# The causal mask of a row-maximum pass, added on TensorE with 64-column identities and 16-bit constants

## The chip, the cores and the metric

The kernel runs on one core of one Trainium2 chip. The metric is the device time of one execution in microseconds (us). Before the change it is 672.27 us, the median of three runs (671.01 to 672.72).

## The reference, cut to what matters

The layer mixes two branches by a per-token gate. Branch A is attention over 2048 tokens in four segments of 512, with 32 heads of 20 channels; within a segment it is causal softmax attention, and across segments a memory of keys and values is read. Branch B sends one token through a feed-forward network. What the change touches is the causal logits:

```python
mask = (ar[:, None] < ar[None, :]).astype(x.dtype) * (-1e9)
logits = jnp.einsum("bhqd,bhkd->bhqk", qs, ks) * scale + mask
p = _softmax(logits, axis=-1)
a_dot = jnp.einsum("bhqk,bhkd->bhqd", p, vs)
```

Softmax needs the maximum of each row of the masked logits. Key j is hidden from query i when i < j.

## The kernel before, in words

Work is cut into 8 units (two halves of the heads, `NU`, times four segments) and each unit into four groups of four heads, so 32 groups n. Per unit, `projections` makes the keys, queries and values by products of split operands (a high and a low part in float32r, a 32-bit type that TensorE reads with fewer bits), at line 371 in `pair_up`: two products at a time, one in rows 0 to 63 of the array, one in rows 64 to 127. They go through DRAM (`place`, `place_low`, `bring_back`) into stacked tiles `qs` and `ks`, where two heads lie in each half of the partitions.

For each group there are two passes over the logits, in five steps k = 0 to 4 each (`LOGITS` lists which blocks of 128 queries and how many keys a step has).

- The first pass, `a_step` (line 645), finds the row maxima. TensorE writes the logits of a step, queries on the partitions, into the one PSUM tile `a` (line 653). Then the mask is added for the last 128 keys of each block of queries, where the diagonal lies (lines 656 to 663). VectorE (DVE) reduces `a` to maxima (lines 666 and 670), which frees `a` for the next step. After k = 4, `m_split` and `m_rows` (line 697) turn the negated maxima into two rows that are put beside the queries.
- The second pass, `b_step` (line 710), makes the transposed logits less the maxima (line 717); ScalarE (ACT) takes the exponential (line 721), GpSimd (POOL) clears what lies above the diagonal (line 727), and `pv_step` multiplies by the values (line 742). `norm` (line 769) divides and stores. `memory_read` (line 503), `memory_write` (line 527) and `keys` (line 492) serve the memory.

The mask of a block is a product of two constants. `pick[r, h]` and `tri[r, h]` lie in the partitions of row half r (64 partitions). With q for a query's and t for a key's place in the block, the rows of h stand for queries 64h to 64h + 63: `pick` as weights has a 1 where a row stands for query q, and `tri`, streamed, holds -1e30 where t is beyond the row's query. The two rounds h = 0 and 1 add up to the mask over all 128 queries, and b = 0, 1 are the two halves of the partitions, each with its own PSUM bank. For k = 0, 1 one block is masked (128 columns streamed, line 660), for k = 2, 3, 4 two blocks in one product (256 columns, line 662). So each step has four mask products, with four loads of weights.

The order of the work is made by a planner while the program is written out: it keeps an estimate of each engine's clock (`now`) and chooses the next piece for TensorE from what should be ready (`a_step`, `b_step`, a piece of projection, `pv_step`, chores). Its costs are constants, such as the step of the maxima:

```python
end = pe((0.41, 0.41, 0.49, 0.49, 0.46)[k], free["a"], stack(n))
```

The change leaves these constants as they are. Each engine then runs its instructions in that order.

`constants` (line 103) fills the constant tiles once, near the start, behind the first splits of weights: an iota on POOL gives `jp` (column less partition), and DVE makes `identf` (line 108), `pick` (line 118) and `tri` (line 119) from it. Behind these, in DVE's order, stand the first copy of a projection out of PSUM (line 428) and more splits (line 175).

Of the kernel before, what the change touches and what calls it, by code (L numbers as in the profile page):

```python
# [8 lines left out]
F32R = mybir.dt.float32r  # L9
BF16 = mybir.dt.bfloat16  # L10
I32 = mybir.dt.int32
AF = mybir.ActivationFunctionType
OP = mybir.AluOpType
# [21 lines left out]
NEG = -1e30  # L35
# [17 lines left out]
def sub(ap, off, dims):  # L53
    return bass.AP(tensor=ap.tensor, offset=ap.offset + off, ap=[list(ap.ap[0])] + dims)
# [3 lines left out]
def tile_infini_mod(  # L58
# [12 lines left out]
    nc = tc.nc  # L71
    one = ctx.enter_context(tc.tile_pool(name="one", bufs=1))
# [10 lines left out]
    def f32(t):  # L83
        return t.bitcast(F32)
# [2 lines left out]


    identf = one.tile([128, 128], F32, name="identf")
    pick = one.tile([128, 2, 128], F32R, name="pick")  # L90
    tri = one.tile([128, 2, 128], F32R, name="tri")
    gate = one.tile([128, H], F32, name="gate")
    ogate = one.tile([128, H], F32, name="ogate")
    mask4 = one.tile([GC, 4], F32, name="mask4")
# [8 lines left out]
    def constants():  # L103
        for t in mneg:
            nc.gpsimd.memset(f32(t), 0.0)
        jp = pool.tile([128, 4 * GW], I32, tag="num", bufs=6, name="jp")[:, :128]
        nc.gpsimd.iota(jp, pattern=[[1, 128]], base=0, channel_multiplier=-1)
        nc.vector.tensor_scalar(identf, jp, 0.0, None, op0=OP.is_equal)
        for i, t in enumerate(ks):
            (nc.gpsimd if i % 2 else nc.vector).memset(f32(t), 1.0)  # L110
        for t in va:
            nc.gpsimd.memset(t, 1.0)

        for h in range(2):
            for r in range(2):
                p = slice(64 * r, 64 * r + 64)
                off = 64.0 * (h - r)
                nc.vector.tensor_scalar(pick[p, h], jp[p], off, None, op0=OP.is_equal)
                nc.vector.tensor_scalar(tri[p, h], jp[p], off, NEG, op0=OP.is_gt, op1=OP.mult)
        nc.sync.dma_start(gate, bass.AP(tensor=beta.tensor, offset=beta.offset, ap=[[0, 128], [1, H]]))  # L120
        nc.scalar.activation(gate, gate, AF.Exp, scale=-1.0)
        nc.vector.tensor_scalar(gate, gate, 1.0, None, op0=OP.add)
        nc.vector.reciprocal(gate, gate)
        nc.vector.tensor_scalar(ogate, gate, -1.0, 1.0, op0=OP.mult, op1=OP.add)

        jd = pool.tile([128, 4 * GW], I32, tag="num", bufs=6, name="jd")[:GC, :GC].rearrange("p (a b) -> p a b", a=4)
        nc.gpsimd.iota(jd, pattern=[[1, 4], [4, DH]], base=0, channel_multiplier=-1)
        ed = pool.tile([128, 4 * GW], F32, tag="num", bufs=6, name="ed")[:GC, :GC].rearrange("p (a b) -> p a b", a=4)
        nc.vector.tensor_scalar(ed, jd, 0.0, None, op0=OP.is_equal)
        nc.vector.tensor_reduce(out=mask4, in_=ed, axis=AX.X, op=OP.max)  # L130
        run("POOL", 4.5)
        run("DVE", 5.5)
# [4 lines left out]
    def run(engine, us, *ready):  # L137
        now[engine] = max([now[engine], *(r + 0.12 for r in ready)]) + us
        return now[engine]

    def pe(us, *ready):
        now["PE"] = max([now["PE"], *ready]) + us
        return now["PE"] + 0.22
# [196 lines left out]
    def use(m):  # L340
        if mode[0] != m:
            mode[0] = m
            pe(0.22)
# [301 lines left out]
    def a_step(n, k):  # L645
        use((64, 128))
        if n not in mx:
            mx[n] = pool.tile([128, 2, 2, 4], F32, tag="mx", bufs=3, name="mx")
        a = psum.tile([128, 2, 512], F32, tag="a", bufs=1, name="a")
        for i, p, at, w in LOGITS[k]:  # L650
            for b in range(2):
                q_ = qs[n % NS][64 * b:64 * b + ST, p, 128 * i:128 * i + 128]
                nc.tensor.matmul(a[:, b, at:at + w], q_, ks[n % NS][64 * b:64 * b + ST, p, :w],  # L653
                                 start=(i, p) == LOGITS[k][0][:2], stop=False)
        ends = [at + w - 128 for i, p, at, w in LOGITS[k]]
        for h in range(2):
            for b in range(2):
                r = slice(64 * b, 64 * b + 64)
                if k < 2:
                    nc.tensor.matmul(a[:, b, ends[0]:], pick[r, h], tri[r, h], start=False, stop=h == 1)  # L660
                else:
                    nc.tensor.matmul(sub(a[:, b], min(ends), [[max(ends) - min(ends), 2], [1, 128]]), pick[r, h],  # L662
                                     sub(tri[r, h], 0, [[0, 2], [1, 128]]), start=False, stop=h == 1)
        end = pe((0.41, 0.41, 0.49, 0.49, 0.46)[k], free["a"], stack(n))
        if k == 4:
            nc.vector.tensor_reduce(out=mx[n][:, :, :, 1], in_=a.rearrange("p b (c t) -> p b c t", c=2), axis=AX.X, op=OP.max)  # L666
            end = run("DVE", 0.16 + 2 / 0.96 * 0.512, end)
        else:
            for i, p, at, w in LOGITS[k]:
                nc.vector.tensor_reduce(out=mx[n][:, :, p, i:i + 1], in_=a[:, :, at:at + w], axis=AX.X, op=OP.max)  # L670
                end = run("DVE", 0.16 + w / 480, end)
        free["a"] = end + 0.1
        done_a[0] += 1
        if k == 4:
            m_split(n)

    def stack(n):
        return max(landed.get(("q", n), 1e9), landed.get(("k", n), 1e9))

    def m_split(n):  # L680
        m = mx.pop(n).rearrange("p b c i -> p b (c i)")
        t = mneg[n % 2]
        hi, lo = sub(t, 0, [[16, 2], [1, 8]]), sub(t, 8, [[16, 2], [1, 8]])
        nc.vector.tensor_scalar(hi, m, -1.0, None, op0=OP.mult)
        nc.vector.scalar_tensor_tensor(out=lo, in0=m, scalar=-1.0, in1=f32(hi), op0=OP.mult, op1=OP.subtract)  # L685
        rows.append((run("DVE", 0.5), n))
# [418 lines left out]
    def logits(ahead, t):  # L1105

        best = None
        for fn, e in ((a_step, next_a()), (b_step, next_b())):
            if e and e[1] <= t and e[0] + LEAD <= chunks[0] + ahead and (best is None or e[0] < best[1][0]):
                best = fn, e  # L1110
        if best is None:
            return False
        fn, e = best
        if fn is b_step:
            b_no[0] += 1
        fn(e[2], e[3])
        return True
# [21 lines left out]
    for _ in range(9):  # L1139
        split_next()  # L1140
    constants()
    now["PE"] = at["T", 0, 0]
    last_side = [0.0]
# [94 lines left out]
```

## Time and profile before

| What | Value |
|---|---|
| median of three runs | 672.27 us |
| profiled execution | 670.66 us |
| its span, first to last instruction | 668.3 us |
| granted TensorE clock | 0.984 |
| TensorE matmuls busy | 618.0 us |
| TensorE weight loads busy | 497.9 us |
| VectorE, ScalarE, GpSimd busy | 401.5, 366.6, 278.3 us |

How to read it: PE is TensorE's matmuls, PEld its weight loads, which overlap them; DVE, ACT, POOL and SP are VectorE, ScalarE, GpSimd and SyncE. A row of groups gives the line, the engine, the operation, the tiles written and read, the shape, the count, then the busy time in us and the mean duration of one in ns, then the idle time of the engine before them and what ended it. A shape such as 64*128 64x256 is 64 rows of the array by 128 columns of weights, with 64 partitions by 256 elements streamed or written. A row of the timeline gives the start and the duration in us, and merges like instructions that follow each other (x4). Matmuls overlap, so that a duration is a latency; what a product costs is read from the distance between starts.

### The profile page before, as it was taken

To read this page: it belongs to the slowest core of one execution; us is meant where nothing else is said; L and a number is where in the kernel's file an instruction comes from. 1 tells how busy PE (TensorE), PEld (TensorE's weight loads), DVE (VectorE), ACT (ScalarE), POOL (GpSimd) and SP (SyncE) were. 2 spreads that over 40 slices of the span, in tenths; PEclk is the share of its full clock that TensorE was granted. 3 is DMA by queue.
4 is the path that set the end of the run, shared out by engine and by line. 5 is a ranking of instruction groups with operands and counts; after the bars stand their busy time and mean duration, and the time that the engine had idled before them with its cause. 6 is when DMAs were issued, how large, how long until landed. Compare 5 with 4: busy or idle time off the path is not lost.

```text
span 668.3 us, 17482 instructions
## 1 busy us (share of the span) xinstructions
PE 618.0 (92%) x6996; PEld 497.9 (75%) x6996; DVE 401.5 (60%) x675; ACT 366.6 (55%) x638; POOL 278.3 (42%) x350
## 2 busy tenths in 40 slices
PE   4589899999999889899999999999999999999996
PEld 3478777788887676776777787777777788787785
DVE  6635665656765747665647684766667676663332
ACT  6452575556756665576346744656465555555331
POOL 5443332633454645554423436343457433232211
PEclk9799989999999979899999999999999999999999
DMA  6598557345642677488847884578625793344451
GB/s 178 163 268 232 162 137 221 101 121 162 168 107 73 196 213 186 135 264 260 258 140 228 260 217 130 144 230 246 192 59 160 222 277 94 116 140 135 140 182 60
DMA packets 81319, 116.55 MB, mean 174 GB/s; under 512 B 36112, under 2 KB 41752, under 8 KB 81240
## 3 DMA queue, kind: packets, MB, share of 16 engines
q1 hardware_dynamic: 81240, 115.46, 59.5%
q8 instruction: 55, 0.90, 0.6%
q14 instruction: 24, 0.20, 0.1%
HBM read 72.94 MB, written 41.96 MB: 172 GB/s over the span
## 4 chain that ended last, share of the span: by engine, by line
PE 73%; DVE 10%; DMA 6%; issue 4%; SPq 2%; ACT 2%; POOL 2%; POOLq 0%; ACTq 0%; DVEq 0%
PE sums L371 23%; PE sumt L371 14%; PE pv L742 10%; PE a L653 5%; PE bt L717 5%; PE a L662 4%; PE nm L503 3%; SPq L147 2%; PE otp L769 2%; DVE mx L666 2%; DMA stkk<-lo 2%; PE mp L527 2%; DMA stkk<-hi 2%; PE a L660 1%; DVE mneg L685 1%
## 5 line engine op out<-in xcount | busy, mean ns | idle before, releaser
L721 ACT ACTIVATE p<-bt 128x1024 f32<-128x1024 f32 x160 | 164.4, 1028 | 73.3 <-PE bt L717 72.0
L670 DVE TENSOR_REDUCE mx<-a 128x2 f32<-128x768 f32 (+1 forms) x192 | 160.6, 865 | 68.0 <-PE a L662 43.9
L727 POOL TENSOR_SCALAR_AFFINE_SELECT p<-p 128x512 f32<-128x512 f32 (+1 forms) x160 | 88.9, 556 | 181.3 <-ACT p L721 173.1
L371 PE MATMUL sums<-xhi,whi 64*128 64x512 f32 (+1 forms) x240 | 91.5, 381 | 12.9 <-ACT xhi L172 8.8
L371 PE MATMUL sumt<-xhi,whi 64*128 64x512 f32 (+1 forms) x240 | 92.0, 384 | 6.2 <-DVE phi L428 6.2
L371 PE MATMUL sums<-xhi,wlo 64*128 64x512 f32 (+1 forms) x240 | 88.8, 370 | 0.0
L371 PE MATMUL sums<-xlo,whi 64*128 64x512 f32 (+1 forms) x240 | 88.3, 368 | 0.1
L371 PE MATMUL sumt<-xhi,wlo 64*128 64x512 f32 (+1 forms) x240 | 88.2, 368 | 0.0
L371 PE MATMUL sumt<-xlo,whi 64*128 64x512 f32 (+1 forms) x240 | 88.2, 368 | 0.0
L717 PE MATMUL bt<-qs,ks 62*128 62x384 f32 (+3 forms) x512 | 73.5, 324 | 8.2 <-ACT p L721 8.1
L742 PE MATMUL pv<-p,va 128*32 128x512 f32 (+3 forms) x1024 | 75.9, 437 | 0.0
L653 PE MATMUL a<-ks,qs 60*128 60x384 f32 (+3 forms) x512 | 73.9, 328 | 0.6 <-DVE mx L666 0.3
L438 POOL TENSOR_TENSOR lo<-phi,hi 128x512 fp32r<-128x512 f32 x40 | 52.3, 1308 | 46.1 <-ACT hi L434 27.5
L717 PEld LDWEIGHTS bt<-qs,ks 62*128 62x128 f32 x512 | 50.3, 188 | 16.7 <-ACT p L721 9.7
L371 PEld LDWEIGHTS sums<-xhi,whi 64*128 64x128 f32 x240 | 45.7, 190 | 22.5 <-ACT xhi L172 8.8
L742 PEld LDWEIGHTS pv<-p,va 128*32 128x32 f32 x1024 | 30.0, 110 | 43.4 <-issue 33.5
L748 ACT COPY pvs<-pv 128x512 f32<-128x512 f32 x32 | 18.8, 586 | 73.8 <-PE pv L742 73.8
L653 PEld LDWEIGHTS a<-ks,qs 60*128 60x128 f32 x512 | 50.2, 189 | 11.6 <-issue 3.4
L666 DVE TENSOR_REDUCE mx<-a 128x4 f32<-128x1024 f32 x32 | 39.2, 1224 | 27.7 <-PE a L662 27.7
L371 PE MATMUL sums<-whi,xhi 64*128 64x322 f32 (+1 forms) x160 | 53.4, 333 | 2.5 <-ACT phi L425 0.7
L371 PE MATMUL sums<-whi,oh 64*128 64x320 f32 x160 | 50.3, 323 | 4.0 <-ACT half L1036 1.4
L371 PE MATMUL sumt<-whi,xhi 64*128 64x322 f32 (+1 forms) x160 | 53.5, 334 | 0.0
(135 smaller groups left out, 1870.4 us busy)
## 6 DMA issues: line engine op xcount, KB each, us to landing
qs<-stkq SPq DMA_DIRECT2D x64, 240.0 KB
ks<-stkk SPq DMA_DIRECT2D x64, 240.0 KB
raw<-in_xT_dram SPq DMA_DIRECT2D x40, 256.0 KB
stkq<-hi SPq DMA_DIRECT2D x32, 320.0 KB
stkq<-lo SPq DMA_DIRECT2D x32, 160.0 KB
otok<-ou SPq DMA_DIRECT2D x32, 160.0 KB
xf<-in_x_dram SPq DMA_DIRECT2D x8, 640.0 KB
out_dram<-xf SPq DMA_DIRECT2D x16, 320.0 KB
```

The lines of the kernel that those rows point to most:

```text
L371: nc.tensor.matmul(o, a, b, start=phase == 0 and i == 0, stop=phase == 1 and i == n - 1)
L438: nc.gpsimd.tensor_tensor(out=lo, in0=c, in1=f32(hi), op=OP.subtract)
L503: nc.tensor.matmul(nm[:, c, :], e[:GC, 128 * c:128 * c + 128], mbd[:, g, :], start=True, stop=True)
L653: nc.tensor.matmul(a[:, b, at:at + w], q_, ks[n % NS][64 * b:64 * b + ST, p, :w], start=(i, p) == LOGITS[k][0][:2], stop=False)
L662: nc.tensor.matmul(sub(a[:, b], min(ends), [[max(ends) - min(ends), 2], [1, 128]]), pick[r, h], sub(tri[r, h], 0, [[0, 2], [1, 128]]), sta ...
L666: nc.vector.tensor_reduce(out=mx[n][:, :, :, 1], in_=a.rearrange("p b (c t) -> p b c t", c=2), axis=AX.X, op=OP.max)
L670: nc.vector.tensor_reduce(out=mx[n][:, :, p, i:i + 1], in_=a[:, :, at:at + w], axis=AX.X, op=OP.max)
L717: nc.tensor.matmul(bt[:, b, at:at + w], k_, qs[n % NS][64 * b:64 * b + ST + 2, p, L - w:], start=True, stop=True)
L721: nc.scalar.activation(pt, bt, AF.Exp, scale=SCALE)
L727: nc.gpsimd.affine_select(out=d, in_=d, pattern=[[0, e[1]] for e in dims[:-1]] + [[1, 128]], base=0, channel_multiplier=-1, compare_op=OP. ...
L742: nc.tensor.matmul(pv[32 * j:32 * j + 32, 128 * c:], va[u % 2][:, c, VW * h:VW * h + 32], pt_tiles[n, j % 2, c][:, j // 2], start=c == 0, ...
L748: nc.scalar.copy(pvs[n], pv)
```

## The change: which constant is the weight, how many columns are streamed, and in which type

The tile `pick` is gone. `eye` is an identity of 64 by 64 in each half of the partitions, `tri` becomes the stationary operand, and both are in bfloat16. In round h the identity is streamed into columns 64h to 64h + 63 of the block alone: with `tri[r, h]` as weights, partition c of the half stands for key 64h + c, and its row holds -1e30 for every query below that key. So the two rounds mask different columns, each for all 128 queries. The count of products and of weight loads is the same; a product streams 64 columns where it was 128, and 128 where it was 256. The constants take two `eye` and four `tri` instructions on DVE, where four `pick` and four `tri` stood.

```diff
     identf = one.tile([128, 128], F32, name="identf")
-    pick = one.tile([128, 2, 128], F32R, name="pick")
-    tri = one.tile([128, 2, 128], F32R, name="tri")
+    tri = one.tile([128, 2, 128], BF16, name="tri")
+    eye = one.tile([128, 64], BF16, name="eye")
...
-        for h in range(2):
-            for r in range(2):
-                p = slice(64 * r, 64 * r + 64)
-                off = 64.0 * (h - r)
-                nc.vector.tensor_scalar(pick[p, h], jp[p], off, None, op0=OP.is_equal)
-                nc.vector.tensor_scalar(tri[p, h], jp[p], off, NEG, op0=OP.is_gt, op1=OP.mult)
+
+        for r in range(2):
+            p = slice(64 * r, 64 * r + 64)
+            nc.vector.tensor_scalar(eye[p], jp[p, :64], -64.0 * r, None, op0=OP.is_equal)
+            for h in range(2):
+                nc.vector.tensor_scalar(tri[p, h], jp[p], 64.0 * (h - r), NEG, op0=OP.is_lt, op1=OP.mult)
...
                 if k < 2:
-                    nc.tensor.matmul(a[:, b, ends[0]:], pick[r, h], tri[r, h], start=False, stop=h == 1)
+                    nc.tensor.matmul(a[:, b, ends[0] + 64 * h:ends[0] + 64 * h + 64], tri[r, h], eye[r], start=False, stop=h == 1)
                 else:
-                    nc.tensor.matmul(sub(a[:, b], min(ends), [[max(ends) - min(ends), 2], [1, 128]]), pick[r, h],
-                                     sub(tri[r, h], 0, [[0, 2], [1, 128]]), start=False, stop=h == 1)
+                    nc.tensor.matmul(sub(a[:, b], min(ends) + 64 * h, [[max(ends) - min(ends), 2], [1, 64]]), tri[r, h],
+                                     sub(eye[r], 0, [[0, 2], [1, 64]]), start=False, stop=h == 1)
```

## The prediction, made before the changed kernel was run

> **What bounds the kernel now.** I read the page first: busy shares, then the chain that ended last.
>
> ```profile
> PE 618.0 (92%) x6996; PEld 497.9 (75%) x6996; DVE 401.5 (60%) x675; ACT 366.6 (55%) x638; POOL 278.3 (42%) x350
> ...
> PE 73%; DVE 10%; DMA 6%; issue 4%; SPq 2%; ACT 2%; POOL 2%; POOLq 0%; ACTq 0%; DVEq 0%
> PE sums L371 23%; PE sumt L371 14%; PE pv L742 10%; PE a L653 5%; PE bt L717 5%; PE a L662 4%; PE nm L503 3%; SPq L147 2%; PE otp L769 2%; DVE mx L666 2%; DMA stkk<-lo 2%; PE mp L527 2%; DMA stkk<-hi 2%; PE a L660 1%; DVE mneg L685 1%
> ```
>
> TensorE is the bound: it carries 73% of the chain, and no other engine is near full. The mask products (L660 and L662) hold 1% and 4% of the chain. So I next ask what one mask product costs, from the groups by form.
>
> ```profile
> L662 PE MATMUL a<-tri,pick 64*128 64x256 f32 x384 | 44.7, 297 | 0.0
> L666 DVE TENSOR_REDUCE mx<-a 128x4 f32<-128x1024 f32 x32 | 39.2, 1224 | 27.7 <-PE a L662 27.7
> L662 PEld LDWEIGHTS a<-tri,pick 64*128 64x128 f32 x384 | 32.2, 189 | 0.0
> L660 PEld LDWEIGHTS a<-tri,pick 64*128 64x128 f32 x256 | 27.2, 190 | 2.5
> L660 PE MATMUL a<-tri,pick 64*128 64x128 f32 x256 | 23.7, 248 | 0.0
> L503 PEld LDWEIGHTS nm<-mbd,phi 80*128 80x128 f32 x192 | 23.2, 192 | 2.8 <-issue 2.2 <-ACT neg L448 0.2
> L527 PEld LDWEIGHTS mp<-va,kk 128*80 128x80 f32 x192 | 14.5, 149 | 1.0 <-issue 1.0
> L492 PEld LDWEIGHTS ktp<-identf,phi 64*128 64x128 f32 x144 | 12.0, 140 | 5.5 <-issue 2.6 <-DVE phi L455 1.6
> ```
>
> Four mask products belong to a step of the maxima, so 256/4 = 64 steps take the narrow form (k = 0, 1) and 384/4 = 96 the wide one; L666 counts the 32 of these with k = 4. The means of 248 and 297 ns are latencies of overlapped instructions, not what a product adds. That is read from the distance between starts, here on a wide step (k = 2 or 3) and then on a narrow one; PEld rows are weight loads.
>
> ```profile
> 111.14 0.41 PE L653 MATMUL a<-ks,qs 60*128 60x384 f32 x4
> 111.32 0.30 PEld L662 LDWEIGHTS a<-tri,pick 64*128 64x128 f32 x4
> 111.38 0.45 PE L662 MATMUL a<-tri,pick 64*128 64x256 f32 x4
> 111.55 0.19 PEld L371 LDWEIGHTS sums<-wlo,xhi 64*128 64x128 f32 x1
> ...
> 111.67 0.31 PE L371 MATMUL sums<-wlo,xhi 64*128 64x322 f32 x1
> ```
>
> ```profile
> 108.77 0.45 PE L653 MATMUL a<-ks,qs 60*128 60x512 f32 x2
> ...
> 108.82 0.43 PEld L660 LDWEIGHTS a<-tri,pick 64*128 64x128 f32 x4
> 109.06 0.34 PE L660 MATMUL a<-tri,pick 64*128 64x128 f32 x4
> ...
> 109.23 0.24 PE L492 MATMUL ktp<-identf,phi 64*128 64x64 f32 x1
> ```
>
> The four products run as two rounds, since the two row halves of the array work side by side. The wide masks hold the array from 111.38 to 111.67, 0.29 us; the narrow ones from 109.06 to 109.23, 0.17 us. Two loads are in each half's line: the second mask's, which starts only when the first mask's matmul has the array, and that of whatever follows. The next fence gives the pace of pure streaming, and that of small products.
>
> ```profile
> 299.79 0.28 PE L371 MATMUL sumt<-xhi,wlo 64*128 64x256 f32 x1
> ...
> 299.91 0.28 PE L371 MATMUL sumt<-xlo,whi 64*128 64x256 f32 x1
> ```
>
> ```profile
> 72.70 1.12 PE L503 MATMUL nm<-mbd,phi 80*128 80x84 f32 x8
> ```
>
> ```profile
> 60.01 2.55 PE L527 MATMUL mp<-va,kk 128*80 128x84 f32 x32
> ```
>
> ```profile
> 309.10 0.40 PE L492 MATMUL ktp<-identf,phi 64*128 64x64 f32 x4
> ```
>
> 256 columns stream in 0.12 us, so 128 in 0.06 and 64 in 0.03. The eight nm products start (1.12 - 0.28)/7 = 0.12 us apart, the mp products (2.55 - 0.24)/31 = 0.075, with the same 84 moving columns but 128 against 80 weight columns. So the load paces nm: 0.045 us for 48 columns, some 0.9 ns a column, and about 0.11 us for 128 columns. I use 0.107, which also fits the two loads per narrow step (0.17 us for 0.12 of streaming). The transposes at L492 load 128 columns too, but take 140 ns in latency instead of 189 and start (0.40 - 0.23)/3 = 0.057 us apart: a load of 128 columns can also be about half as long.
>
> **The change, part by part.** The number of mask products and of their weight loads stays at 640, in the same order, with no new wait: the planner's costs are untouched, so every engine keeps its order and nothing is moved past a queue. Each product streams half the columns (64 for 128, 128 for 256). Weights become tri, 128 columns as before, in 16 bits. The two h rounds now write different columns instead of adding on the same ones.
>
> What a shorter stream is worth hangs on the load, and no load of 16-bit weights is in this trace. Bounds: as dear as today's, 0.107 us; or as the transposes', about 0.053. I take 0.053: half the bytes for the same columns, and the trace has that pace for 128 columns. The sum, in ns, each product waiting for its load and for the product before it:
>
> - Narrow step, from the first mask on: today the second mask's load and the next product's load, 107 + 107 = 214. After: 53 + 107 = 160. Saved 54; with a dear load, 0, since loads alone set the pace.
> - Wide step with k = 2 or 3, from the start of its 128-column L653 product (111.32): today 107 + 118 + 118 = 343, and the rows give 111.67 - 111.32 = 0.35 us. After: 58 + 58 + 107 = 223. Saved 120; with a dear load 3 x 107 = 321, saved 22.
> - Wide step with k = 4, from its second 256-column L653 product: today 118 x 3 = 354. After: 118 + 58 + 107 = 283, saved 71; dear load: 118 + 107 + 107 = 332, saved 22.
>
> Sum: 64 x 54 + 64 x 120 + 32 x 71 = 13.4 us. Dear load: 96 x 22 = 2.1 us. A load that costs nothing adds at most 64 x 24 = 1.5 us (a narrow round then lasts its 64 columns, 29 ns), 15.0 in all.
>
> [...] No row here shows a 16-bit load.
>
> How much of it reaches the end: mask products hold 5% of the chain by the rounded page, at least 4.5%, so 30 us of the span. All mask stretches together are 64 x 0.17 + 64 x 0.29 + 32 x 0.24 = 37 us. So 0.81 of each saved us lies on the chain: 10.8 us.
>
> The constants change as well: on DVE eight instructions become six.
>
> ```profile
> 12.84 4.17 DVE L108 TENSOR_SCALAR identf<-jp 128x128 f32<-128x128 int32 x1
> ...
> 17.00 4.14 DVE L119 TENSOR_SCALAR tri<-jp 64x128 fp32r<-64x128 int32 x1
> 21.15 0.23 DVE L118 TENSOR_SCALAR pick<-jp 64x128 fp32r<-64x128 int32 x1
> ...
> 22.03 0.22 DVE L119 TENSOR_SCALAR tri<-jp 64x128 fp32r<-64x128 int32 x1
> ...
> 24.83 0.68 DVE L428 COPY phi<-sumt 128x512 f32<-128x512 f32 x1
> ```
>
> ```profile
> 19.78 1.27 POOL L438 TENSOR_TENSOR lo<-phi,hi 128x512 fp32r<-128x512 f32 x1
> ```
>
> ```profile
> 25.56 0.79 PE L371 MATMUL sumt<-xhi,whi 64*128 64x512 f32 x1 [6.24 <-DVE phi L428]
> ```
>
> One tri instruction lasts 4.14 us; it ends at 21.14, right after POOL's unbroken work ends at 21.05, so it sat behind POOL. The six others take 22.25 - 21.15 = 1.10 us, and TensorE waits 6.24 us for the copy behind them. The stall ends with POOL's work and stays. If again the second instruction is caught, four are left behind it instead of six: 4 x 0.18 = 0.73, saved 0.37 us. By where the stall falls: 0.18 (first caught) to 0.55 (third); that is all on TensorE's wait. I take 0.4.
>
> Sum 10.8 + 0.4 = 11.2. I keep 10, because a chain that is shortened lets other waits come last. These are the ones that TensorE shows:
>
> ```profile
> PE bt L717 <- ACT p L721: 8.1, 5, 5.2
> ...
> PE mtp L697 <- DVE mneg L685: 5.3, 7, 1.0
> ```
>
> Both end with another engine and grow if TensorE arrives sooner; ~1 us of 13 is a choice, not a reading. The profiled execution took 670.66 us (span 668.3), 1.6 below the median of the runs, 672.27. Minus 10: 660.7 or 662.3. I predict 661.5.
>
> **The rivals.**
> - *The load stays dear* (0.107 us for 16 bits too): saved 2.1 x 0.81 + 0.4 = 2.1 us, 668.6 to 670.2. For it: all plain 32-bit loads in the trace have this pace. Against: the transposes.
> - *Slower: a change of type empties the array.* A change of the tile's shape does so today:
>
> ```profile
> 304.88 0.27 PE L371 MATMUL sums<-xlo,whi 64*128 64x256 f32 x1
> ...
> 305.09 0.66 PE L769 MATMUL otp<-identf,pvs 128*128 128x128 f32 x4
> ```
>
> ```profile
> 307.96 0.28 PE L371 MATMUL sums<-xlo,whi 64*128 64x256 f32 x1
> 307.98 0.41 PE L492 MATMUL ktp<-identf,phi 64*128 64x64 f32 x6
> ```
>
> The first pair is 0.21 us apart where 256 columns take 0.12: 0.09 us lost. If going to 16 bits and back cost that, 160 steps would lose 2 x 160 x 0.09 = 28.8 us against 13.4 saved: 15 slower, 686. It turns slower from 13.4/320 = 0.042 us a change. Against it: in the second pair the f32 transposes follow a 32-bit-reduced product in the same tile shape without a gap.
> - *The saving is eaten elsewhere*: if DVE's reductions or the round trips by DMA come last throughout, about 1 us is left, 669.7 to 671.3. For it: single buffer a, which each reduction must free. Against: TensorE's own waits for the reductions (L670, L666) are not among its larger ones, and DVE is 60% busy.
>
> **How the numbers follow.** A measurement can tell about 0.3% (2.0 us) from no change. Forecast (cheap load, 6 to 15 us saved) 0.64; dear load 0.16, half of it beyond 0.3%; eaten 0.08; slower 0.12. So faster 0.64 + 0.08 = 0.72, within 0.3% 0.08 + 0.08 = 0.16, slower 0.12. The range runs from 15.0 + 0.55 saved on the profiled time, rounded to 655.5, to 671.0, which takes in the dear load and leaves out the slower case and some of the eaten one.
>
> **What would show it.** The loads of L660 and L662 should fall from 190 ns to about 140 or less; at 190 the dear load holds. From the first wide mask to the next product 0.29 us should become about 0.17, on the narrow step 0.17 about 0.12. A gap of near 0.09 us before or behind the masks would show the drain. The first maxima step should come about 0.4 us earlier by the constants. If the mask stretches shrink by 13 us and the time by much less, the waits at L717 and L697 must have grown. The forecast is wrong if the load keeps its length, or if the carried share of 0.81 does.

## The result, and the profile after

The changed kernel takes 664.57 us (median of six runs, 659.86 to 668.84) against 672.50 us before (six runs, 671.01 to 674.37). The ratio is 0.9886, with a 95% interval of 0.9851 to 0.9922: 7.7 us, or 1.1%, less. In two later comparisons the same kernel gave 0.9862 (0.9829 to 0.9896) and 0.9889 (0.9850 to 0.9928). So the saving is 7.5 to 9.3 us, by these three; it is taken from the ratios here and below, and the medians alone lie 7.9, 9.9 and 8.8 us apart. The profiled execution took 659.86 us, with a span of 657.9.

The page of the changed kernel, with busy shares and the chain:

```profile
PE 605.9 (92%) x6996; PEld 473.9 (72%) x6996; DVE 399.6 (61%) x673; ACT 366.6 (56%) x638; POOL 278.8 (42%) x350
...
PE 72%; DVE 10%; issue 5%; DMA 4%; ACT 4%; SPq 3%; POOL 2%; POOLq 0%; ACTq 0%; DVEq 0%
PE sums L371 26%; PE sumt L371 12%; PE pv L742 10%; PE bt L717 6%; PE a L653 5%; SPq L147 3%; PE nm L503 3%; PE otp L769 2%; PE mp L527 2%; DVE mx L666 2%; PE a L662 2%; DVE mneg L685 1%; PE ttp L964 1%; ACT p L721 1%; DMA stkk<-lo 1%
```

TensorE still bounds the kernel. Of the mask products, L662 has gone from 4% to 2% of the chain, and L660 has left the list. The groups by form show the new products and loads:

```profile
L662 PE MATMUL a<-eye,tri 64*128 64x128 bf16 x384 | 30.4, 223 | 0.0
L660 PE MATMUL a<-eye,tri 64*128 64x64 bf16 x256 | 17.2, 197 | 0.0
L662 PEld LDWEIGHTS <-tri 64*128 64x128 bf16 x384 | 13.4, 96 | 3.2
```

The load of 128 columns has fallen from 189 ns to 96, below the 140 ns of the transposes' loads that the prediction leaned on. The same wide step as in the prediction, and a narrow one, from the timeline of the changed kernel:

```profile
109.00 0.40 PE L653 MATMUL a<-ks,qs 60*128 60x384 f32 x4
109.23 0.12 PEld L662 LDWEIGHTS <-tri 64*128 64x128 bf16 x4
109.24 0.29 PE L662 MATMUL a<-eye,tri 64*128 64x128 bf16 x4
109.31 0.19 PEld L371 LDWEIGHTS sums<-wlo,xhi 64*128 64x128 f32 x1
...
109.33 0.40 PE L371 MATMUL sums<-wlo,xhi 64*128 64x322 f32 x1
...
109.57 0.30 PE L371 MATMUL sums<-whi,xlo 64*128 64x322 f32 x1
```

```profile
106.64 0.46 PE L653 MATMUL a<-ks,qs 60*128 60x512 f32 x2
106.93 0.24 PE L660 MATMUL a<-eye,tri 64*128 64x64 bf16 x4
107.00 0.31 PE L492 MATMUL ktp<-identf,phi 64*128 64x64 f32 x2
```

The wide masks start at 109.24 and the next product at 109.33, but that start seems to be stamped too early. The product lasts 0.40 us where its successor lasts 0.30, and the load of its own 32-bit weights began only at 109.31, so it must have waited for them. So a step is better measured to the second product behind the mask. From the first L653 product that is 109.57 - 109.00 = 0.57 us, against 0.67 before; these rows give the latter:

```profile
111.14 0.41 PE L653 MATMUL a<-ks,qs 60*128 60x384 f32 x4
...
111.81 0.31 PE L371 MATMUL sums<-whi,xlo 64*128 64x322 f32 x1
```

### The profile page after: what moved, and what is told of

Read it like the earlier page. It is cut to its first block, busy times and chain, and to the rows that moved or that the text cites. A ratio compares the mean times of both kernels' runs of the same rounds, so it can differ in the third digit from the quotient of the medians.

```text
span 657.9 us, 17480 instructions
## 1 busy us (share of the span) xinstructions
PE 605.9 (92%) x6996; PEld 473.9 (72%) x6996; DVE 399.6 (61%) x673; ACT 366.6 (56%) x638; POOL 278.8 (42%) x350
## 4 chain that ended last, share of the span: by engine, by line
PE 72%; DVE 10%; issue 5%; DMA 4%; ACT 4%; SPq 3%; POOL 2%; POOLq 0%; ACTq 0%; DVEq 0%
PE sums L371 26%; PE sumt L371 12%; PE pv L742 10%; PE bt L717 6%; PE a L653 5%; SPq L147 3%; PE nm L503 3%; PE otp L769 2%; PE mp L527 2%; DVE mx L666 2%; PE a L662 2%; DVE mneg L685 1%; PE ttp L964 1%; ACT p L721 1%; DMA stkk<-lo 1%
## 5 line engine op out<-in xcount | busy, mean ns | idle before, releaser
L727 POOL TENSOR_SCALAR_AFFINE_SELECT p<-p 128x512 f32<-128x512 f32 (+1 forms) x160 | 90.7, 567 | 175.5 <-ACT p L721 167.7
L371 PE MATMUL sums<-xhi,whi 64*128 64x512 f32 (+1 forms) x240 | 92.9, 387 | 13.9 <-ACT xhi L172 8.9
L371 PE MATMUL sumt<-xhi,whi 64*128 64x512 f32 (+1 forms) x240 | 93.5, 390 | 5.0 <-DVE phi L428 5.0
L371 PE MATMUL sums<-xhi,wlo 64*128 64x512 f32 (+1 forms) x240 | 90.4, 377 | 0.0
L371 PE MATMUL sumt<-xhi,wlo 64*128 64x512 f32 (+1 forms) x240 | 90.1, 375 | 0.0
L717 PE MATMUL bt<-qs,ks 62*128 62x384 f32 (+3 forms) x512 | 76.4, 335 | 8.5 <-ACT p L721 8.3
L653 PE MATMUL a<-ks,qs 60*128 60x384 f32 (+3 forms) x512 | 74.2, 328 | 1.5 <-DVE mx L670 1.0
L653 PEld LDWEIGHTS a<-ks,qs 60*128 60x128 f32 x512 | 50.0, 188 | 12.8 <-issue 3.6
```

The lines of the kernel that those rows point to most:

```text
L371: nc.tensor.matmul(o, a, b, start=phase == 0 and i == 0, stop=phase == 1 and i == n - 1)
L717: nc.tensor.matmul(bt[:, b, at:at + w], k_, qs[n % NS][64 * b:64 * b + ST + 2, p, L - w:], start=True, stop=True)
L727: nc.gpsimd.affine_select(out=d, in_=d, pattern=[[0, e[1]] for e in dims[:-1]] + [[1, 128]], base=0, channel_multiplier=-1, compare_op=OP. ...
```

## The experiments

**One half of the change at a time.** First the type alone.

```diff
-    pick = one.tile([128, 2, 128], F32R, name="pick")
-    tri = one.tile([128, 2, 128], F32R, name="tri")
+    pick = one.tile([128, 2, 128], BF16, name="pick")
+    tri = one.tile([128, 2, 128], BF16, name="tri")
```

> The form of before (identity as weights, 128 or 256 columns streamed), but both constants in 16 bits. Theory A (weight loads and streamed columns each set the pace in turn, and about 0.8 of what a mask stretch loses reaches the end): with loads of 16 bits at 96 ns latency the narrow steps lose 0.05 us each, the wide ones with k = 2, 3 0.05, those with k = 4 nothing, 6.3 us in all, about 5 at the end: 667.5 us. Theory B (the type alone brings it all): as the changed kernel, 662 to 665. Theory C (the masks are off the path; the gain is the shorter constants and a luckier phase): within 1 us of before.

Measured: 668.14 us against 672.68, ratio 0.9933 (0.9902 to 0.9964), 4.5 us less. Its timeline on the same step, and its load:

```profile
109.51 0.40 PE L653 MATMUL a<-ks,qs 60*128 60x384 f32 x4
109.75 0.39 PE L662 MATMUL a<-tri,pick 64*128 64x256 bf16 x4
109.90 0.39 PE L371 MATMUL sums<-wlo,xhi 64*128 64x322 f32 x1
...
110.13 0.31 PE L371 MATMUL sums<-whi,xlo 64*128 64x322 f32 x1
```

```profile
L662 PEld LDWEIGHTS <-pick 64*128 64x128 bf16 x384 | 13.4, 96 | 3.2
```

The step takes 110.13 - 109.51 = 0.62 us, 0.05 less than before, as theory A had it. Now the columns alone.

```diff
-    tri = one.tile([128, 2, 128], BF16, name="tri")
-    eye = one.tile([128, 64], BF16, name="eye")
+    tri = one.tile([128, 2, 128], F32R, name="tri")
+    eye = one.tile([128, 64], F32R, name="eye")
```

> The changed form (64 or 128 columns streamed, triangles as weights), but both constants in the 32-bit type of before. Theory A: loads of 107 ns set the pace again; the narrow steps gain nothing, the wide ones 0.02 us each, 2.1 us, and 0.4 by the constants: about 2 us less than before, 670.5. Theory B: only the constants' 0.4. Theory D (the halved columns bring it all): as the changed kernel, 662 to 665.

Measured: 669.17 us against 672.68, ratio 0.9963 (0.9938 to 0.9988), by the ratio 2.5 us less.

```profile
111.93 0.41 PE L653 MATMUL a<-ks,qs 60*128 60x384 f32 x4
112.17 0.39 PE L662 MATMUL a<-eye,tri 64*128 64x128 f32 x4
112.39 0.36 PE L371 MATMUL sums<-wlo,xhi 64*128 64x322 f32 x1
...
112.59 0.30 PE L371 MATMUL sums<-whi,xlo 64*128 64x322 f32 x1
```

```profile
L662 PEld LDWEIGHTS a<-eye,tri 64*128 64x128 f32 x384 | 31.9, 188 | 0.0
```

The step takes 0.66 us, 0.01 less than before: the loads set the pace (the two rounds take 112.39 - 112.17 = 0.22 us, where their columns stream in 2 x 0.06), and half the columns are worth little. Theories B (type alone) and D (columns alone) both fall. Their intervals lie apart from that of the changed kernel in the same comparison (0.9829 to 0.9896); in its two other comparisons that one reaches up to 0.9922 and 0.9928 and meets the lower end of type alone, so against theory B the steps count too. 4.5 + 2.5 = 7.0 us is below the 9.3 that the whole gave there, and by the steps too the two halves together give more than their sum.

**The changed kernel again**, for the spread of its runs.

> The changed kernel again, for the spread of its runs. If the granted clock makes the spread, its slower runs show the lower clocks, about 9 us for 0.010 of the mean clock; if the order of waits makes it, time and clock are not tied. Median 8 to 11 us below before.

> The changed kernel once more, as the base for the other two on the same chip: 8 to 10 us below before. If the granted clock is part of what is lost, its mean clock is again some 0.002 to 0.003 under that of before.

Measured: 662.82 us (ratio 0.9862) and 662.94 us (ratio 0.9889). Over its 18 runs the mean granted clock is 0.9796 (0.972 to 0.985), over 54 runs of the kernel before 0.9834 (0.977 to 0.990). In both, slower runs have lower clocks: a fitted line gives 6.1 us for 0.010 of clock in the one (correlation -0.80) and 4.5 in the other (-0.65), less than the 9 us expected. So time and clock are tied, and the changed kernel is granted about 0.004 less, worth some 2 us by these lines.

**More and less of the same.** The mask of the maxima left out, and the mask made twice:

```diff
-                                 start=(i, p) == LOGITS[k][0][:2], stop=False)
-        ends = [at + w - 128 for i, p, at, w in LOGITS[k]]
-        for h in range(2):
-            for b in range(2):
...
+                                 start=True, stop=True)
```

> The changed kernel with the mask of the maxima left out (all four mask products of each step; the maxima are then over unmasked logits). Theory A: what is left of a mask stretch in the changed kernel, some 0.12 to 0.14 us a step, goes as well, about 20 us over 160 steps, 0.8 of it at the end: 16 us below the changed kernel, about 647. If TensorE's saving no longer reaches the end (other engines come last), under 6 us below the changed kernel. Theory C (masks off the path): no more than 1 us.

Measured: 651.06 us against 671.40, ratio 0.9701 (0.9659 to 0.9743). That is 20 us below before and, by the three ratios of the changed kernel, 11 to 13 below that one, not 16.

```diff
-        for h in range(2):
+        for i, h in enumerate((0, 1, 0, 1)):
...
-                    nc.tensor.matmul(..., tri[r, h], eye[r], start=False, stop=h == 1)
+                    nc.tensor.matmul(..., tri[r, h], eye[r], start=False, stop=i == 3)
```

> The changed kernel with every mask product made twice (eight a step). Theory A: the loads of 16 bits are too short to count, so an added round costs its streaming: 2 x 0.03 us on 64 narrow steps and 2 x 0.06 on 96 wide ones, 15.4 us of TensorE's time; 12 us at the end if 0.8 is carried, 15 if all of it is. Were a load of 16 bits as dear as half of 0.107, the narrow steps would pay 2 x 0.053 and the sum be 18. Theory C: under 2 us.

Measured: 671.71 us against 671.40, ratio 1.0003 (0.9972 to 1.0034): 8 to 9.5 us more than the changed kernel, not 12. The steps of the two, without and with the double mask:

```profile
109.44 0.41 PE L653 MATMUL a<-ks,qs 60*128 60x384 f32 x4
109.67 0.36 PE L371 MATMUL sumt<-wlo,xhi 64*128 64x322 f32 x1
...
109.88 0.30 PE L371 MATMUL sumt<-whi,xlo 64*128 64x322 f32 x1
```

```profile
109.31 0.41 PE L653 MATMUL a<-ks,qs 60*128 60x384 f32 x4
109.55 0.41 PE L662 MATMUL a<-eye,tri 64*128 64x128 bf16 x8
109.75 0.39 PE L371 MATMUL sums<-wlo,xhi 64*128 64x322 f32 x1
...
109.99 0.30 PE L371 MATMUL sums<-whi,xlo 64*128 64x322 f32 x1
```

The steps take 0.44 and 0.68 us, around the 0.57 of the changed kernel. An added pair of wide rounds costs 0.11 us, which is its streaming (2 x 0.06): a load of 16 bits does not count beside it.

I took the same distance for each step that projections follow without a break, to the end of the fourth product of a pair stream, and compared medians. The table has one form of each kind of step, over some 5 to 8 steps each; other forms gave other values (three narrow steps in front of projections of 256 columns gained nothing). So the sums in the fifth column, 64 x narrow + 64 x wide + 32 x (k = 4), take every step as an undisturbed one. The column "paired" goes by two profiled executions, product by product, as TensorE's order is the same in both: over all steps it adds up how much sooner the fourth product behind the masks starts, counted from the step's first L653 product. The last column is what the runs gave.

| Against before, ns a step | narrow | k = 2, 3 | k = 4 | sum, us | paired, us | runs, us |
|---|---|---|---|---|---|---|
| type alone | -45 | -42 | +3 | -5.5 | -5.4 | -4.5 |
| columns alone | +2 | -6 | -17 | -0.8 | -2.6 | -2.5 |
| both (the change) | -72 | -96 | -56 | -12.5 | -11.6 | -7.5 to -9.3 |
| no mask | -215 | -244 | -240 | -37.1 | -28.9 | -20.1 |

| Against the change | narrow | k = 2, 3 | k = 4 | sum, us | paired, us | runs, us |
|---|---|---|---|---|---|---|
| mask twice | +62 | +101 | +112 | +14.0 | +11.5 | +8 to +9.5 |

Paired, the two other profiles of the changed kernel give 10.4 and 11.4 us. By the sums, less would reach the end the more TensorE saves: 12.5 us give 8 or 9, 37 give 20. By the pairs that is hardly so: 4.5 of 5.4, 7.5 to 9.3 of 11.6, 8 to 9.5 of 11.5 and 20.1 of 28.9 us, about 0.65 to 0.83 each time. Of the 17 us that are missing from the 37, 8 were never gained in the steps. The pairs rest on one profile of each kernel, so these shares are rough.

Part of what is lost outside the steps goes with the clock. In the profiles of the kernel before, of the changed kernel and of that without the mask, the granted clock drops to 0.50 in some stretches, most of them 3.4 or 6.8 us long: five before, five in the changed kernel and eight in that without the mask. These rows show one stretch of the changed kernel, its full clock behind it, and one stretch of the kernel without the mask. A row has the window and its length, the busy times of PE, PEld, DVE, ACT and POOL, then the clock, the share of the DMA engines and GB/s:

```profile
82.00:85.00 3.00, 3.00 (x26) 2.39 (x25) 1.74 (x4) 1.72 (x3) 0.95 (x2) 0.50 0.94 235
86.00:228.00 142.00, 136.27 (x1672) 107.37 (x1664) 93.57 (x158) 90.42 (x158) 66.56 (x88) 1.00 0.52 144
```

```profile
122.00:124.50 2.50, 2.50 (x16) 2.13 (x16) 0.44 (x2) 0.76 (x1) 1.60 (x2) 0.50 0.27 92
```

The mean clock of the no-mask kernel's runs is 0.9767, 0.007 under before; that of the double mask is 0.9841. An estimate from the mean clocks and spans: half clock takes some 22 us of a run before, 27 in the changed kernel and 30 without the mask. At most half of such time is lost (in the changed kernel's stretch from 23.8 us, products of 512 columns start 0.43 us apart, against 0.23 at 17.7 to 18.4), so of what is missing at the end this explains at most some 2.5 us in the changed kernel and 4 us in that without the mask. But the clock does not simply follow the work of TensorE: type alone, which saves work, has 0.9835, and three kernels below with the products of the changed one have 0.9828, 0.9860 and 0.9769.

What brings such a stretch on is not shown. In the 3.4 us ahead of the one at 82 (78.4 to 81.8) TensorE was busy for 1.72 us and idle for the rest. That waits cause the lower clock is the author's guess from this.

**The constants at the start.** VectorE's identity, triangles and gates were moved behind the first copies out of PSUM, in one piece, and then in two (the identity behind the first copies, the rest behind the second).

```diff
-        nc.vector.tensor_scalar(identf, jp, 0.0, None, op0=OP.is_equal)
+        late.append(jp)
...
+        if late and u == 0 and j == 1:
+            late_constants()
```

> The changed kernel with all of VectorE's constants but the fills (identity, triangles, eye, gates, the memory's mask) written behind the first copies of a projection out of PSUM instead of ahead of them; the planner's clock is charged as before, so TensorE's order stays. Theory A: the wait of 4 to 5 us for that copy is on the chain; it falls below 1 us and the kernel gets 3 to 5 us faster than the changed one, about 658.5. Rival: the next wait (splits, the stacks' way through DRAM) takes its place, and the time stays within 1 us.

> The changed kernel with VectorE's identity for transposes written behind the first copies of a projection out of PSUM, and the triangles, eye, gates and the memory's mask behind the second ones; the planner is charged as before. Theory A: both waits of the start (for the copy, and the 3 us for the keys' transposes that the constants behind the first copies brought) fall below 1 us, and 3 to 5 us less than the changed kernel are left at the end. Rival: as with the constants moved in one piece, the next wait at the start takes their place, and the time stays within 1.5 us of the changed kernel.

Measured: 661.36 us, ratio 0.9861 (0.9823 to 0.9900), and 659.64 us, ratio 0.9856 (0.9803 to 0.9909). By the ratios, neither can be told from the changed kernel (0.9862 and 0.9889). The second's median lies 3.3 us under that of the changed kernel in the same comparison (662.94), as theory A had it; but its runs were granted more clock, 0.9860 against 0.9787, worth 3 to 4 us by the fitted lines. In the profiles the wait for the copy is gone from both. In the first, a wait of 3.1 us for the keys' transposes took its place. In the second the longest of these is 2.0 us (6.7 in all, against 6.1 in the first and 2.4 in the changed kernel), and the 151st projection product starts at 32.5 us, against 38.6 in the changed kernel; yet the 241st starts at 47.0 against 48.1. The lead ends in the waits of its start:

```profile
45.36 0.31 PE L504 MATMUL ktp<-identf,phi 64*128 64x64 f32 x2 [2.00 <-DVE phi L467]
```

```profile
DVE phi L467 <- POOL lo L450: 5.4, 1, 5.4
...
POOL lo L450 <- ACT hi L446: 5.0, 1, 5.0
ACT hi L446 <- DMA stkk<-hi: 4.2, 1, 4.2
```

Read upward: a transfer to the stacks holds a tile of ACT, then POOL, then VectorE, then TensorE's transposes (L504 is L492 in the changed kernel). So in the profiles the rival holds: behind the constants' wait stands that chain through DRAM. The times leave open whether up to some 3 us were won.

Without the mask and without its constants, on top of the split constants:

> The mask of the maxima left out and its constants with it, on top of the split constants (the maxima are over unmasked logits). If the two savings add up: 11 us for the mask and 0 to 4 for the constants below the changed kernel, 648 to 651. If both meet the same waits, no less than 651, the kernel without mask before.

Measured: 650.35 us, ratio 0.9690 (0.9644 to 0.9736), not to be told from the no-mask kernel's 0.9701, so it does not decide between the two cases. Both no-mask kernels beat the changed one. They rest on the inputs, because a maximum over more keys cancels in the division only while the exponents stay in range.

**The planner's costs.**

```diff
-        end = pe((0.41, 0.41, 0.49, 0.49, 0.46)[k], free["a"], stack(n))
+        end = pe((0.38, 0.38, 0.43, 0.43, 0.42)[k], free["a"], stack(n))
```

> The changed kernel with the planner's cost of a maxima step lowered towards what it is now (0.38, 0.38, 0.43, 0.43, 0.42 in place of 0.41, 0.41, 0.49, 0.49, 0.46). If the old costs leave waits in the order that a fitting cost would take out, 2 to 4 us less than the changed kernel; if the order is as good as any, within 2 us either way.

Measured: 664.84 us against 671.40, ratio 0.9907 (0.9881 to 0.9934); not faster than the changed kernel. TensorE's waits for ACT's exponentials grew from 8.3 us in the changed kernel:

```profile
PE bt L717 <- ACT p L721: 13.9, 8, 5.5
```

So the old costs left no order to be gained by this step; other values were not run.

## Why the prediction was right, point by point

The forecast was 661.5 us, 10 less than before; 7.5 to 9.3 us less were measured. The range alone says little, as it takes in the dear load too (its lower end should read 655.1, which is 670.66 - 15.55). That the time fell for the stated reason rests on the loads and on the experiments.

- *The bound*: right. What the change saves comes from TensorE's mask stretches: its busy time fell by 12 us, that of the other engines moved by 2 us at most, and the number of products stayed.
- *The price of a 16-bit load*, the choice on which all hung: the right end, but still too dear. Taken at 0.053 us, it shows at 96 ns of latency, and doubling the masks adds the streaming alone. With 128 columns as before, the loads of the mask went from 189 ns in float32r to 96 in bfloat16, while loads of 128 columns that stayed in 32 bits kept theirs (L503: 192 ns before, 191 after). The 0.107 us taken for a 32-bit load is near what columns alone gave, 0.11 us a round.
- *The steps*: the term that was mis-sized. 54, 120 and 71 ns were forecast, 72, 96 and 56 measured on undisturbed steps; in sum 13.4 and 12.5 us, and 11.6 by the pairs. That the sums come so near is in part luck, as the errors have opposite signs. The narrow step gained more because the load is shorter (in the double mask, two more narrow rounds cost 62 ns, no more than their streaming). The wide ones gained less: the first round of 128 columns lasts 0.067 us (start to start) instead of 0.058, and by the stamps the first load of the 16-bit weights starts at 109.23, 0.05 us after the product before it, where a 32-bit one starts with that product (111.32 and 111.32 before). Why it starts later is not shown.
- *The share that reaches the end*: about right, after the deduction. 0.81 was read from the chain, and 1 us was taken off by choice, which leaves 10 of 13.8 us, 0.72. The runs gave 7.5 to 9.3 of the 11.6 us by the pairs, 0.65 to 0.80. (The least that the rounded page allows for the masks is 4.0% of the chain, not 4.5; unrounded, the trace has 4.8.) The chain tells what ended last in that execution, not what comes next when it is shortened. The two waits that were named grew by 1.1 us together:

```profile
PE bt L717 <- ACT p L721: 8.3, 5, 5.2
PE mtp L697 <- DVE mneg L685: 6.2, 9, 1.1
```

  That is the size of the deduction, but as much or more can have gone with the lower clock, and the two are not separated.
- *The constants*: 0.4 us forecast. VectorE was caught behind POOL twice rather than once, for about as long in all, and fewer instructions were left to run freely:

```profile
17.07 3.05 DVE L119 TENSOR_SCALAR tri<-jp 64x128 bf16<-64x128 int32 x2
20.14 0.19 DVE L117 TENSOR_SCALAR eye<-jp 64x64 bf16<-64x64 int32 x1
20.25 1.43 DVE L119 TENSOR_SCALAR tri<-jp 64x128 bf16<-64x128 int32 x2
...
24.26 0.68 DVE L428 COPY phi<-sumt 128x512 f32<-128x512 f32 x1
```

  POOL worked from 17.23 to 19.91 and from 20.14 to 21.45 meanwhile. The copy came at 24.26 instead of 24.83, 0.6 us sooner. That this was "all on TensorE's wait" was true, and that it reached the end was not shown: with the split constants a lead of 6 us had shrunk to 1 us by the 241st projection product. The first product of the maxima came 0.9 us earlier than before (47.2 for 48.1), but with the type alone, which has all eight instructions, it came at 47.3.
- *The rivals*: the dear load falls with the type alone. The drain at a change of type falls too: type alone has 320 such changes and is faster. "Eaten elsewhere" is true in part, for a fifth to a third of what the steps gained.

## What to carry to other kernels

In these traces a product on a row half of the array costs the longer of its streaming and the next load (with columns alone 0.11 us a round, where 128 columns stream in 0.06), so look for the load first: half the columns alone won 2.5 us, half the bytes alone 4.5, and both 7.5 to 9.3. Constants that need no more than 16 bits belong in 16 bits, as the load fell from 189 ns to 96 here: the identity is exact in them, and the -1e30 need not be. A saving read from the chain is a forecast of one execution: it gave 0.81, and runs with more and with less of the same work gave 0.65 to 0.83. But what the steps gain has to be taken over all steps, not from the undisturbed ones alone.

## What the runs showed of the hardware that was not expected

- The load of 128 columns of 16-bit weights takes 96 ns against 189 in 32 bits, and in the double mask it does not show beside the streaming (0.11 us for two rounds).
- The granted clock drops to 0.50 for stretches of some 3 to 7 us several times in an execution, on one core: five in the profile before, five in that of the change, eight in that without the mask. Ahead of one of them TensorE was busy for 1.72 of 3.4 us. The mean over the runs is 0.9834 before, 0.9796 with the change and 0.9767 without the mask, but 0.9835 with the type alone and 0.9860 with the split constants, so less work for TensorE does not settle it.
